# A fused top-k attention and PReLU MLP kernel on one core: one Exp for two duos, score copies two slots ahead, the factor 1 - alpha moved to the Relu, and a new order of the drain

## The chip, the cores and the metric

The kernel runs on one core of one Trainium2 chip. The metric is the device time of one execution in microseconds (us); three runs of the kernel before gave 814.25, 814.66 and 815.23 us, median 814.66. The profile shows one further execution, which took 814.44 us. Engines are named as in the profile: PE (matrix multiply; PEld its weight loads), DVE (vector), ACT (scalar), POOL (GpSimd) and SP (which issues most DMAs; SPq is its queue).

## The reference

Eight batches of eight heads, 576 tokens, head size 64. Each score row keeps its 32 largest entries, the result goes through a two-layer MLP with a PReLU whose slope alpha differs by feature.

```python
def _attn_ref(q, k, v):                       # q, k, v: (8, 8, 576, 64) float32
    scores = scale * np.matmul(q, k.transpose(0, 1, 3, 2))
    kth = np.partition(scores, -top_k, axis=-1)[..., -top_k:-top_k + 1]   # top_k = 32
    scores = np.where(scores >= kth, scores, -1000000000.0)
    attn = np.exp(scores - np.max(scores, axis=-1, keepdims=True))
    attn = attn / (np.sum(attn, axis=-1, keepdims=True) + 1e-09)
    return np.matmul(attn, v).astype(np.float32)

def _moe_ref(x, w_in, w_out, alpha):          # x: (4608, 512), w_in: (512, 2048), w_out: (2048, 512)
    h = x @ w_in
    g = np.maximum(h, 0.0) + alpha * np.minimum(h, 0.0)
    return (g @ w_out).astype(np.float32)
```

## The kernel before

**Work and slots.** Two heads form a pair. The score rows are cut into 144 duos (the list `duos`, lines 77 to 91), each of two tiles of 128 rows by 576 scores: mostly one tile of each head of a pair ("n"), and for the last 64 rows of the heads, one tile of two heads each ("m"). The main loop (lines 736 to 792) runs 144 slots, one per duo; slot n issues one stage for each of several duos, so that the stages of a duo lie slots apart. `stage` (lines 360 to 371) holds the lags. A pair of slots here is an even slot and the odd one after it, and belongs to two duos whose thresholds are found together.

**The stages of duo n.** PE multiplies q by k into the PSUM tile `ps_sc` (`st_qk`, one buffer); ACT copies it to SBUF as `s_sb` (`st_exit`). In slot n DVE takes the eight largest of each of six groups of 96 scores per row (the search, 12 MAX8, results `up` and, in the PSUM tile `small`, `lo`). In odd slots `threshold_steps` folds these for both duos (`fold`, `negate`, `least`, `turn`) into a first threshold `p9`. In slot n + 2 ACT makes the signs against it with a count (`st_count`, tile `sg`), POOL multiplies them with the scores (`st_y`, tile `y`), and DVE takes the next eight with a MAX8 over 576 (`row`, which also writes into `p9`). In slot n + 4 `pick_steps` chooses the exact threshold `KT` from the count, ACT computes Exp (`st_exp`, tile `w`) and the signs against `KT` (`st_cut`, tile `f`), POOL multiplies `w` by `f`, and SP issues a DMA that transposes `w` into `wT`. In slot n + 7 (n + 8 early on) PE multiplies `wT` by v into `xo` (`st_av`), and for each two duos DVE divides by the row sums (`norm_a`, `norm_b`, tile `x`), and SP transposes `x` into `xT`.

**The MLP.** `mlp_ready` cuts finished tokens into units. A unit multiplies `xT` by `w_in_b` into `ph` (`h_pe`), `h_relu` takes Relu of it into `gT`, and parts (`o_pe`) multiply `gT` by `w_out_b` into `pz`, together with `xT` by `w_lin_b`. Since PReLU is alpha h + (1 - alpha) Relu(h), `w_lin_b` is w_in alpha w_out, built in slots 16 to 24, and `w_out_b` carries the factor 1 - alpha: `scale_out` (lines 636 to 644) scales each of its 16 blocks on ACT. `o_act` copies `pz` out, `o_sp` stores it. `keep_warm` fills PE with idle products.

**Order.** Each engine runs its instructions in the order in which this loop issues them (class `Ordered`; all records of the trace carry its line 32, so that groups are told by tile). Only DVE's small steps on the tile `small` float between their neighbours. So a wait at the head of an engine's queue holds all that stands behind it. In a slot ACT has: two signs `sg` with their count reads, sometimes a copy of `pz`, the Exp, two signs `f`, the score copy, sometimes a copy of transposed q or k (`qkT`). The tiles `sg` and `f` share three buffers, `s_sb` has six, `w` four, `wT` three.

**The drain.** After slot 143 the stages that are left are written out by hand (lines 830 to 906), and a loop (907 to 922) empties the MLP, with Relus taken by DVE and ACT in turn. A last check (`check_low`) sets a flag; if it is set, a general path (not run here) repeats the work.

Of the kernel before, what the change touches and what calls it, by code (L numbers as in the profile page):

```python
# [8 lines left out]
FP32 = mybir.dt.float32  # L9
# [8 lines left out]
NG = 6  # L18

# [40 lines left out]
def fast_path(tc, q, k, v, moe_w_in, moe_w_out, moe_alpha, out, flag):  # L60
# [16 lines left out]
    duos = []  # L77
# [15 lines left out]
    with ExitStack() as ctx:  # L93
# [5 lines left out]
        s_p = pool("s", 6)  # L99
# [47 lines left out]
        def sm(ins, reads, writes):  # L147
# [8 lines left out]
            DVE.small.add(ins.ins.name)  # L156
            recent.append((ins.ins, reads, writes))
            del recent[:-60]
# [10 lines left out]
        ws = [const.tile([128, 2, 640], BF16, name=f"w_{i}") for i in range(4)]  # L169
# [3 lines left out]
        alpha1m = const.tile([128, NFT], FP32, name="alpha1m")  # L173
        w_lin_b = [const.tile([128, DMODEL], BF16, name=f"w_lin_b{i}") for i in range(4)]
# [6 lines left out]
        for t in ws:  # L181
            POOL.memset(t[:, :, S:640], 0.0)
# [134 lines left out]
        def dve_slot(n, f_late):  # L317

            norm = norm_of(n)
            rows = duos_at("count", n)  # L320
# [15 lines left out]
            turn = None  # L336
            if n % 2:
                fold, negate, least, turn = threshold_steps(n // 2)
                fold()
                if n < ND - 1:  # L340
                    h_relu()
                negate()
            else:
                h_relu()
            for d in rows:
                row(d, 0)
            if turn:
                least()
                turn()
            if norm:  # L350
                norm_a(norm)
            for d in rows:
                row(d, 1)
            if norm:
                norm_b(norm)
            if f_late:
                h_pe()
                h_relu()
# [6 lines left out]
        for d in range(ND):  # L365
            for kind, lag in (("count", 2), ("cut", 4), ("exp", 4), ("av", 8 if d < 13 else 7)):
                stage.setdefault((kind, d + lag), []).append(d)
        for m in range(ND // 2):
            stage["pick", 2 * m + 4] = [m]
        for d in range(1, ND, 2):  # L370
            stage["norm", d + (8 if d < 13 else 7)] = d

        def st_count(n, rows=(0, 1)):
            s, p9 = T["s", n], T["p9", n // 2]
            if rows[0] == 0:
                T["sg", n] = two.tile([128, 2, S], BF16, name="sg", tag="sg", bufs=3)
                if n % 2 == 0:
                    T["cs", n // 2] = three.tile([128, 4], FP32, name="cs", tag="cs")
            sg, cs = T["sg", n], T["cs", n // 2]
            for i in rows:  # L380
                r = 2 * (n % 2) + i
                ACT.activation(sg[:, i, :], s[:, i, :], AF.Sign, bias=p9[:, r, 0:1], scale=-1.0,
                               accum_out=cs[:, r:r + 1])

        def st_y(n):
            y = two.tile([128, 2, S], FP32, name="y", tag="y")
            sg = T.pop(("sg", n))
            for i in range(2):
                POOL.tensor_tensor(y[:, i, :], T["s", n][:, i, :], sg[:, i, :], ALU.mult)
            T["y", n] = y  # L390
# [4 lines left out]
        def st_cut(n):  # L395
            w, s = ws[n % 4][:, :, 0:S], T.pop(("s", n))
            f = two.tile([128, 2, S], mybir.dt.uint8, name="f", tag="sg", bufs=3)
            for i in range(2):
                ACT.activation(f[:, i, :], s[:, i, :], AF.Sign, bias=KT[:, 2 * n + i:2 * n + i + 1])
# [163 lines left out]
        def h_relu(eng=None):  # L563
            if act:
                ch, f0, e_n, ph = act.pop(0)
                if eng is ACT:
                    ACT.activation(ch["g"][:, f0:f0 + e_n, :], ph, AF.Relu)
                else:
                    DVE.tensor_scalar(ch["g"][:, f0:f0 + e_n, :], ph, 0.0, None, ALU.max)
# [66 lines left out]
        def scale_out(f):  # L636
            if f % 8 == 0:
                hold["wl", f // 8] = gp.tile([128, 8, 512], BF16, name="w_la", tag="gT")
            src = hold["st", f // 4][:, f % 4, :]
            ACT.activation(w_out_b[f // 4][:, f % 4, :], src, AF.Copy, scale=alpha1m[:, f:f + 1])  # L640

            sm(DVE.tensor_tensor(hold["wl", f // 8][:, f % 8, :], src,
                                 alpha_ps[:, f:f + 1].to_broadcast([128, 512]), ALU.mult),
               [(304 + f, 305 + f)], [])
# [91 lines left out]
        for n in range(ND):  # L736
            now[0] = n
            run(n, "kd")
            o_sp()

            if n > 4 and not h_pe():
                keep_warm()
            wide_copy = n % 2 and (n, "prep") in todo
            if n > 3:
                run(n, "prep", 1)
            if n and on(n + 1):
                st_qk(n + 1)
            if n < 4:
                run(n, "prep", 2)
            if 0 < n < 5:  # L750
                keep_warm()
            for m in duos_at("av", n):
                st_av(m)
            late = len(hq) > (9 if n < 118 else 4 if n < 132 else 3) and n % 2 == 0 and not (on(n + 1) and duos[n + 1][0] == "m")

            for m in duos_at("count", n):
                st_count(m)
                st_y(m)
            if ready() > 4 or not wide_copy:
                o_act()  # L760
            for m in duos_at("exp", n):
                st_exp(m)
            if not norm_of(n):
                run(n, "ld")
            run(n, "lin_out")
            did = o_pe()
            run(n, "w")

            dve_slot(n, late)
            for m in duos_at("cut", n):  # L770
                st_cut(m)
            if n and on(n + 1):
                st_exit(n + 1)
            run(n, "cast")
            if (n, "lin") in todo:
                run(n, "lin")
            elif not ready() > (2 if n < 128 else 1) or on(n + 2) and duos[n + 2][0] == "m" or not o_pe():
                if n and not did:
                    keep_warm()
            while pend:  # L780
                short = len(pend[0][0].shape) == 3
                wide = pend[0][0].shape[1] == 512
                on_dve = n > 3 and (short and n > 16 or wide and (n < 17 or n % 2 == 0))
                prep_evac(DVE.tensor_copy if on_dve else ACT.copy)
            if n == 1:
                sm(DVE.tensor_copy(alpha_ps, aps), [], [(304, 320)])
                ACT.activation(alpha1m, aps, AF.Copy, scale=-1.0, bias=1.0)
            run(n, "scale")
            if norm_of(n):
                st_xT(norm_of(n) - 1)  # L790
                st_xT(norm_of(n))
                run(n, "ld")
# [42 lines left out]
        o_sp()  # L835
        st_av(D - 6)
        h_pe(2)
        h_relu(ACT)
        h_pe(2)
        h_relu(ACT)  # L840
        o_act()
        o_sp()
        st_count(D - 1)
        st_y(D - 1)
        picked(D // 2 - 1)
        normed(D - 6)
        h_relu()
        st_count(D)
        st_y(D)
        st_exp(D - 3)  # L850
        st_cut(D - 3)
        st_exp(D - 2)
        row(D - 1, 0)
        now[0] += 1
        o_pe()
        st_av(D - 5)
        o_pe()
        h_pe(2)
        o_pe()
        row(D - 1, 1)  # L860
        h_relu()
        h_pe(2)
        st_av(D - 4)
        row(D, 0)
        row(D, 1)
        st_cut(D - 2)
        picked(D // 2)
        normed(D - 4)
        st_exp(D - 1)
        h_relu(ACT)  # L870
        o_act()
        o_sp()
        h_pe(2)
        o_pe()
        st_exp(D)
        h_relu(ACT)
        st_mask(D - 1)
        st_mask(D)
        st_wT(D - 2)
        o_pe()  # L880
        o_pe()
        o_act()
        o_sp()
        for _ in range(2):
            h_pe(2)
            h_relu(ACT)
        ps = turn_w(D)
        st_av(D - 3)
        turned(D, ps)
        h_pe(2)  # L890
        h_relu(ACT)
        st_av(D - 1)
        st_av(D)
        norm_a(D)
        norm_b(D)
        h_pe(2)
        h_relu(ACT)
        st_av(D - 2)
        normed(D - 2)
        st_xT(D)  # L900
        now[0] += 2
        o_pe()
        o_pe()
        o_pe()
        o_act()
        o_sp()
        turn = 0
        while hq or act or soon or oq or stores:
# [4 lines left out]
            h_relu((DVE, ACT)[turn % 2])  # L913
            turn += 1
            if turn == 1:
                check_low()
            o_act()
            o_sp()
            if not hq and not act:
                o_pe()  # L920
                o_act()
# [282 lines left out]
```

## Time and profile before

| view | value |
|---|---|
| median of three runs | 814.66 us |
| the profiled execution | 814.44 us |
| its span in the trace | 812.4 us |
| busy share of the span | PE 90%, DVE 93%, ACT 94%, POOL 88% |
| clock granted to PE | 0.994 |

The span is from the first to the last instruction; 2.0 us of the execution lie outside it. A busy time counts each instant once, however many records overlap. Groups of instructions are given with count, busy time and mean duration, and with the idle time of the engine ahead of them and what ended it. Two ACT instructions that follow each other without a wait overlap in their records, so the time that one costs is the distance to the start of the next, about 0.1 us less than its record. In the trace slot 2 begins at 17.7 us, slot 18 at 105.9 and slot 142 at 761.7 (first `sg` of the slot).

### The profile page before, as it was taken

The numbers are of one execution on the slowest core, as the hardware profiler recorded it, in microseconds if no ns is written. First come the engines' busy times: TensorE is split into PE (matmuls) and PEld (weight loads), VectorE is DVE, ScalarE is ACT, GpSimd is POOL, SyncE is SP. The second block draws the span as 40 slices with busy tenths as digits, with TensorE's granted clock in tenths as the row PEclk, the third lists the DMA queues.
The fourth block names the chain that finished last, engine by engine and source line by source line (L and its number), as shares of the span: only waits on it lengthen the run. The fifth ranks groups of instructions, "written<-read, shape, count | busy, mean of one in ns | idle before, by whom it ended". The sixth has DMA issues, their size and how long they took to land.

```text
span 812.4 us, 17847 instructions
## 1 busy us (share of the span) xinstructions
PE 734.3 (90%) x5375; PEld 421.4 (52%) x5448; DVE 755.8 (93%) x3470; ACT 767.0 (94%) x1265; POOL 713.6 (88%) x565
## 2 busy tenths in 40 slices
PE   8888899989989998889989989898989999999886
PEld 5333455545545555555545555454545555556563
DVE  4999999999999999999999999999999999999961
ACT  5999999999999999999999999999999999999971
POOL 2898899999999999989999999999999988998860
PEclk9999999999999999999999999999999999999999
DMA  7799976665565575655576555665566565544361
GB/s 153 196 176 173 178 145 133 115 118 116 124 121 122 113 124 120 127 122 105 127 140 117 129 110 124 108 123 117 119 136 116 116 134 100 99 99 89 82 114 37
DMA packets 342327, 99.90 MB, mean 123 GB/s; under 512 B 336128, under 2 KB 336400, under 8 KB 342224
## 3 DMA queue, kind: packets, MB, share of 16 engines
q1 hardware_dynamic: 338928, 91.18, 58.0%
q0 software_dynamic: 1952, 7.09, 3.7%
q8 instruction: 45, 0.74, 0.4%
q10 hardware_dynamic: 1344, 0.43, 0.2%
q14 instruction: 58, 0.48, 0.2%
HBM read 36.71 MB, written 9.44 MB: 57 GB/s over the span
## 4 chain that ended last, share of the span: by engine, by line
DVE 33%; PE 22%; ACT 18%; POOL 12%; issue 10%; SPq 2%; DMA 2%; ACTq 0%; POOLq 0%; DVEq 0%
DVE small L32 11%; PE ps_sc L32 7%; DVE p L32 7%; POOL y L32 7%; DVE up L32 6%; PE pz L32 5%; ACT f L32 5%; ACT sg L32 4%; ACT s_sb L32 4%; POOL w L32 4%; PE ph L32 4%; DVE gT L32 4%; PE xo L32 3%; ACT w L32 3%; SPq L32 2%
## 5 line engine op out<-in xcount | busy, mean ns | idle before, releaser
L32 POOL TENSOR_TENSOR y<-s_sb,sg 128x576 f32<-128x576 f32 x288 | 362.2, 1279 | 25.2 <-ACT sg L32 24.5
L32 POOL TENSOR_TENSOR w<-w,f 128x1152 bf16<-128x1152 bf16 x142 | 317.8, 2238 | 45.8 <-ACT f L32 44.1
L32 ACT ACTIVATE sg<-s_sb,p 128x576 bf16<-128x576 f32 x288 | 221.6, 774 | 10.6 <-DVE p L32 8.3
L32 DVE MAX8 up<-s_sb 128x8 f32<-128x96 f32 x864 | 212.1, 245 | 11.0 <-ACT s_sb L32 10.9
L32 DVE MAX8 p<-y 128x8 f32<-128x576 f32 x288 | 215.0, 748 | 7.3 <-POOL y L32 6.4
L32 DVE MAX8 small<-s_sb 128x8 f32<-128x96 f32 x864 | 216.2, 250 | 0.0
L32 ACT ACTIVATE f<-s_sb,KZ 128x576 uint8<-128x576 f32 x284 | 203.8, 769 | 0.0
L32 PE MATMUL ps_sc<-qkT 64*128 64x512 f32 (+2 forms) x768 | 183.0, 566 | 22.9 <-ACT s_sb L32 22.5
L32 ACT ACTIVATE w<-s_sb 128x1152 bf16<-128x1152 f32 x144 | 166.9, 1159 | 0.0
L32 ACT COPY s_sb<-ps_sc 128x1152 f32<-128x1152 f32 x144 | 159.2, 1106 | 5.8 <-PE ps_sc L32 5.6
L32 PE MATMUL ph<-xT,w_in_b 128*128 128x256 bf16 (+1 forms) x1472 | 149.6, 249 | 7.0 <-DMA xT<-x 3.1
L32 PE MATMUL pz<-w_out_b,gT 128*128 128x512 bf16 x545 | 142.1, 379 | 9.4 <-issue 6.0
L32 PEld LDWEIGHTS <-w_in_b 128*128 128x128 bf16 x1472 | 119.6, 98 | 50.2 <-issue 10.0
L32 PE MATMUL xo<-v,wT 128*128 128x65 bf16 (+3 forms) x1600 | 126.1, 198 | 0.6 <-DVE x L32 0.6
L32 PEld LDWEIGHTS <-wT 128*128 128x128 bf16 (+3 forms) x1600 | 97.3, 99 | 28.9 <-issue 0.8
L32 DVE TENSOR_SCALAR gT<-ph 128x512 bf16<-128x512 f32 x134 | 90.4, 674 | 8.6 <-PE ph L32 8.6
L32 PEld LDWEIGHTS ps_sc<-qkT 64*128 64x128 f32 (+1 forms) x768 | 55.5, 169 | 66.8 <-ACT s_sb L32 35.0
L32 PEld LDWEIGHTS ps_sc<-kd,qkT 128*128 128x128 f32 x256 | 38.1, 188 | 97.1 <-issue 93.3
L32 PEld LDWEIGHTS <-gT 128*128 128x128 bf16 x576 | 54.6, 98 | 59.1 <-DVE gT L32 4.7
L32 PE MATMUL ps_sc<-kd,qkT 128*128 128x128 f32 x256 | 62.5, 326 | 0.0
L32 PE MATMUL rest<-idle 128*128 128x512 bf16 x200 | 52.5, 389 | 6.6 <-DVE gT L32 4.4
L32 ACT ACTIVATION_READ_ACCUMULATOR sg<-s_sb,p 128x1 f32 x288 | 56.2, 195 | 0.0
(67 smaller groups left out, 569.5 us busy)
## 6 DMA issues: line engine op xcount, KB each, us to landing
k_st<-in_k_dram SPq DMA_DIRECT2D x64, 128.0 KB, 2.8
v_st<-in_v_dram SPq DMA_DIRECT2D x64, 128.0 KB, 2.9
q_st<-in_q_dram SPq DMA_DIRECT2D x62, 128.0 KB, 2.7
out_dram<-o_sb SPq DMA_DIRECT2D x29, 256.0 KB, 2.5
w_st<-in_moe_w_out_dram POOLq DMA_DIRECT2D x4, 1024.0 KB, 7.3
wT<-w SPq DMA_TRANSPOSE x143, 3.5
w_in_b<-in_moe_w_in_dram POOLq DMA_DIRECT2D x4, 512.0 KB, 6.6
k_st<-in_k_dram SPq DMA_DIRECT2D x32, 32.0 KB, 2.6
```

Of the source, the lines that this page charges most:

```text
L32: ins = self.tc.keep_in_program_order(f(*a, **kw))
```

## The change

1. **Exp.** `st_exp` of single duos stays for slots 0 to 17 and for the last two duos. From slot 17 on, each odd slot n has one Exp over duos n - 3 and n - 2 (`exp_two`, 128 x 2304), issued behind the two signs `f`. To make that possible the six buffers of `s_sb` become one tile `s_all`, and the four of `w` two tiles `wp` of two duos each.
2. **Copies.** From slot 8 on (`LEAD`) slot n issues the score products and the copy of duo n + 2 rather than n + 1 (`ahead`); slot 8 issues both.
3. **1 - alpha.** `h_relu` becomes one DVE instruction with two inputs, max(ph, 0) times `alpha1m` (an SBUF column repeated along the tokens); `w_out_b` becomes a plain cast of w_out, 11 blocks on ACT and 5 on POOL (`CS`). ACT's Relus of the drain (10) go to DVE.
4. **Loads.** q is loaded at s0 - 4 rather than s0 - 2 (from batch 2 on), v mostly one slot sooner. The lag of 8 for `st_av` ends at duo 10 rather than 12. The pair before the last is prepared one slot sooner; two wide copies of `qkT` go from ACT to DVE.
5. **Order.** A slot is written as a list of names (`HEAD_E`, `HEAD_O` up to slot 17, then `EVEN`, `ODD`), the drain as `DRAIN`. From slot 18 on `st_av` stands ahead of `st_qk` on PE, the copies of `qkT` stand ahead of the Relu on DVE, and `turn` comes behind both `row` steps. `PM` has no "P", `ROWS` is 999 and `SC` has only "D", so these branches are not taken.

```diff
+LEAD = 8
+CS = "AAPAAPAAPAAPAAPA"
+MODE = 18
+PAIRS = 18
+HEAD_E = "kd osp h prep qk av c0 c1 oact exp ld ope S R r0 na r1 nb late k0 k1 exit cast ope2 evac xt"
+HEAD_O = "kd osp h prep qk av c0 c1 oact exp ld ope S F R N r0 L T na r1 nb late E k0 k1 exit cast ope2 evac xt"
+EVEN = "kd osp h prep av c0 c1 oact ld qk ope S evac R r0 na r1 nb late k0 k1 exit cast ope2 xt"
+DRAIN = "a6 osp h RD h RD oact osp c1 p1 n6 RD op c0 k3 r10 h now op a5 r11 RD h a4 r00 r01 op k2 p0 e1 RD oact n4 osp h op e0 m1 RD m0 w2 op op oact osp h RD h RD tw a3 td h RD a1 a0 na nb RD a2 h n2 now now x0 op op oact osp op now h h RD low op oact osp now h h op RD oact osp now h h op RD osp op op oact oact osp"
+ODD = "kd osp h prep av qk ope c0 c1 oact ld S R F r0 N r1 L T late k0 k1 E evac exit cast ope2 xt"
...
-        ws = [const.tile([128, 2, 640], BF16, name=f"w_{i}") for i in range(4)]
+        wp = [const.tile([128, 4, 640], BF16, name=f"w_{i}") for i in range(2)]
+        ws = [wp[i // 2][:, 2 * (i % 2):2 * (i % 2) + 2, :] for i in range(4)]
+        s_all = const.tile([128, 12, S], FP32, name="s_sb")
...
         def st_exit(n):
-            s = s_p.tile([128, 2, S], FP32, name="s_sb", tag="s")
+            s = s_all[:, 2 * (n % 6):2 * (n % 6) + 2, :]
             ACT.copy(s, two_of(T.pop(("ps", n)), 960, S))
...
-            for kind, lag in (("count", 2), ("cut", 4), ("exp", 4), ("av", 8 if d < 13 else 7)):
+            for kind, lag in (("count", 2), ("cut", 4), ("exp", 4), ("av", 8 if d < MODE - 7 else 7)):
...
+        def exp_two(n):
+            c = 2 * (n % 6)
+            ACT.activation(wp[n // 2 % 2][:, :, 0:S], s_all[:, c:c + 4, :], AF.Exp, scale=att_scale)
...
-                if eng is ACT:
-                    ACT.activation(ch["g"][:, f0:f0 + e_n, :], ph, AF.Relu)
-                else:
-                    DVE.tensor_scalar(ch["g"][:, f0:f0 + e_n, :], ph, 0.0, None, ALU.max)
+                DVE.scalar_tensor_tensor(out=ch["g"][:, f0:f0 + e_n, :], in0=ph, scalar=0.0,
+                                         in1=alpha1m[:, f0:f0 + e_n].unsqueeze(2).to_broadcast(list(ph.shape)),
+                                         op0=ALU.max, op1=ALU.mult)
...
-                s0 = NB * (b - 1) + 4 + 4 * i + (2 if p == NPAIR - 2 else 0)
+                s0 = NB * (b - 1) + 4 + 4 * i + (1 if p == NPAIR - 2 else 0)
                 at(s0 - 3, "ld", lambda p=p: load_one(p, "k"))
-                at(s0 - 2, "ld", lambda p=p: load_one(p, "q"))
+                at(s0 - (2 if b == 1 else 4), "ld", lambda p=p: load_one(p, "q"))
                 early = 2 if b == B - 1 else 0
-                at(s0 + 6 - early, "ld", lambda p=p: load_one(p, "v"))
+                at(s0 + (6 if b == 1 and i < 2 else 5) - early, "ld", lambda p=p: load_one(p, "v"))
...
-            ACT.activation(w_out_b[f // 4][:, f % 4, :], src, AF.Copy, scale=alpha1m[:, f:f + 1])
+            plain = w_out_b[f // 4][:, f % 4, :]
+            if CS[f] == "A":
+                ACT.copy(plain, src)
+            else:
+                POOL.tensor_copy(plain, src)
...
+        def ahead(n):
+            return [m for m in ([n + 1] if n < LEAD else [n + 1, n + 2] if n == LEAD else [n + 2]) if n and on(m)]
...
+            def t_E():
+                if n % 2 and n >= PAIRS - 1 and on(n - 3):
+                    exp_two(n - 3)
...
+            for t in ((HEAD_O if n % 2 else HEAD_E) if n < MODE else ODD if n % 2 else EVEN).split():
+                tok[t]()
...
-        o_sp()
-        st_av(D - 6)
-        h_pe(2)
-        h_relu(ACT)
...
+        for t in DRAIN.split():
+            end[t]()
         while hq or act or soon or oq or stores:
             now[0] += 1
             while h_pe(2):
                 pass
             o_pe()
-            h_relu((DVE, ACT)[turn % 2])
+            h_relu()
```

The names stand for: c0, c1 the count and `y` of one row tile each; k0, k1 the signs `f` and, behind k1, POOL's product and the transpose; exp, E the single and the double Exp; exit the score copy; S the search; F, N, L, T `fold`, `negate`, `least`, `turn`; R and RD the Relu; r0, r1 `row`; na, nb the division; evac the copies of `qkT`; oact, osp copy and store of the output; ope, op a part, h a unit of the MLP; ld, xt the loads and the transposes of `x`. In the drain a number is the duo counted back from the last one (a6 is `st_av` of the last but six, r10 its first row tile of the last but one).

More of the change, by code (lines that the diff above doesn't have):

```diff
@@ L392, in st_exp, with st_cut @@
         def st_exp(n):
             ACT.activation(ws[n % 4][:, :, 0:S], T["s", n], AF.Exp, scale=att_scale)
[L395 to L399, printed above, removed]
+        def st_cut(n, rows=(0, 1)):
+            w, s = ws[n % 4][:, :, 0:S], T["s", n]
+            if rows[0] == 0:
+                T["f", n] = two.tile([128, 2, S], mybir.dt.uint8, name="f", tag="sg", bufs=3)
+            f = T["f", n]
+            for i in rows:
+                kt = KT[:, 2 * n + i:2 * n + i + 1]
+                if i and MODE < now[0] < ND - 4 and PM[now[0] % 18] == "P":
+                    POOL.tensor_scalar(f[:, i, :], s[:, i, :], kt, 0.0, ALU.add, ALU.is_gt)
+                else:
+                    ACT.activation(f[:, i, :], s[:, i, :], AF.Sign, bias=kt)
+            if rows[-1] == 0:
+                return
@@ L734, in fast_path, with evac @@
         PE.transpose(aps, a16, ident_f[0:NFT, 0:NFT])
-        for n in range(ND):
-            now[0] = n
-            run(n, "kd")
-            o_sp()
[L741 to L779, printed above, removed]
+        def ahead(n):
+            return [m for m in ([n + 1] if n < LEAD else [n + 1, n + 2] if n == LEAD else [n + 2]) if n and on(m)]
+        def evac(n):
             while pend:
@@ L782, in fast_path @@
                 wide = pend[0][0].shape[1] == 512
-                on_dve = n > 3 and (short and n > 16 or wide and (n < 17 or n % 2 == 0))
+                on_dve = n > 3 and (short and n > 16 or wide and (EV[n] == "D" if n < 18 else n % 2 == 0))
                 prep_evac(DVE.tensor_copy if on_dve else ACT.copy)
[L785 to L788, printed above, removed]
@@ L794, in picked, with is_late @@
+        def is_late(n):
+            return len(hq) > (9 if n < 118 else 4 if n < 132 else 3) and n % 2 == 0 and not (on(n + 1) and duos[n + 1][0] == "m")
+        for n in range(ND):
+            slot(n)
         def picked(m):
@@ L858, in fast_path @@
[L858 to L907, printed above, removed]
+        turn = []
+        def end_now():
+            now[0] += 1
@@ L912, in fast_path @@
             o_pe()
[L913 to L916 removed]
+            h_relu()
             o_act()
             o_sp()
[L919 to L921 removed]
         o_sp()
```

238 lines of the change are left out of this document (168 added, 70 removed).

## The prediction

> **What bounds the kernel now.** I read the busy shares first, then the stages, then what each engine waits for, then one slot of ACT in order of time.
>
> ```profile
> span 812.4 us, 17847 instructions
> core 0: us, PE busy (x) PEld busy (x) DVE busy (x) ACT busy (x) POOL busy (x), PEclk, DMA share, GB/s
> 20.00:104.00 84.00, 70.67 (x396) 32.74 (x395) 79.99 (x354) 82.43 (x141) 77.08 (x68) 0.96 0.94 179
> 104.00:762.00 658.00, 606.46 (x4486) 351.10 (x4551) 641.04 (x2976) 645.72 (x1056) 610.22 (x454) 1.00 0.60 118
> 762.00:812.40 50.40, 39.33 (x411) 26.15 (x415) 25.79 (x82) 27.13 (x47) 21.67 (x18) 0.97 0.40 76
> ```
>
> The three stretches are the head (slots up to 17), the steady part and the drain. In the steady part ACT is busy 645.7 of 658 us, DVE 641.0, POOL 610.2: ACT idles 12.3 us, DVE 17.0. Two engines are full, and each waits a little for the other:
>
> ```profile
> ACT sg L32 <- DVE p L32: 8.3, 21, 1.7
> DVE up L32 <- ACT s_sb L32: 6.2, 20, 0.7
> DVE gT L32 <- PE ph L32: 2.8, 5, 1.0
> POOL w L32 <- ACT f L32: 40.0, 65, 1.1
> L32 ACT COPY s_sb<-ps_sc 128x1152 f32<-128x1152 f32 x125 | 138.0, 1104 | 1.7 <-PE ps_sc L32 1.5
> L32 ACT COPY o_sb<-pz 128x512 f32<-128x512 f32 x31 | 17.5, 566 | 0.0
> ```
>
> (Wait rows: us in total, times, longest.) ACT's sign waits for `turn`, DVE's search for the score copy. POOL's waits cost nothing by themselves. The 125 score copies give 125 slots, 5.26 us each, 10.53 us for an even and an odd slot, and 62 such pairs of slots.
>
> ```profile
> 310.09 1.10 ACT L32 COPY s_sb<-ps_sc 128x1152 f32<-128x1152 f32 x1
> 311.09 0.78 ACT L32 ACTIVATE sg<-s_sb,p 128x576 bf16<-128x576 f32 x1
> ...
> 312.62 1.15 ACT L32 ACTIVATE w<-s_sb 128x1152 bf16<-128x1152 f32 x1
> 313.67 1.43 ACT L32 ACTIVATE f<-s_sb,KZ 128x576 uint8<-128x576 f32 x2
> 315.00 1.10 ACT L32 COPY s_sb<-ps_sc 128x1152 f32<-128x1152 f32 x1
> ```
>
> From start to start: copy 1.00, two signs `sg` 1.53, Exp 1.05, two signs `f` 1.33 us.
>
> **One Exp for two.** The two copies above have slopes (1104 - 566) / 640 = 0.84 ns per column. An Exp of 2304 columns then takes 1.15 + 1152 x 0.84 ns = 2.12 us of record and some 2.02 to its successor, against 2 x 1.05: 0.08 us saved for a pair of slots, 5 us over 62. The other bound: `f` (1.43 us for two, 0.76 one) and Exp (1.15) give 0.68 ns per column, hence 0.27 us saved, 17 us. I take the copies, which differ only in length, while `f` reads `KZ` besides.
>
> The Trainium skill ("ScalarE: Activation LUTs", What ACT_TABLE_LOAD costs) puts an activation without a pointer operand at 186 ns + 0.833 ns per column, one with a pointer about 93 ns higher, and lets neighbours overlap by some 93 ns. It speaks against the change: only the 93 ns that do not overlap would be saved, 6 us in all, and `f`'s higher record would be its pointer.
>
> **What the copies cost ACT.** In the built program the copy of duo n + 2 waits for the second `f` of duo n - 4, whose buffer it takes. In even slots that `f` is the instruction right in front of it; in odd slots the Exp lies between. Such a wait on a neighbour shows here:
>
> ```profile
> 13.12 0.27 ACT L32 COPY qkT<-tps 128x128 f32<-128x128 f32 x1
> 13.47 0.50 ACT L32 COPY kd<-qkT 64x64 f32<-64x64 f32 x2
> ...
> 312.83 0.24 DVE L32 MAX8 up<-s_sb 128x8 f32<-128x96 f32 x1
> 312.99 0.25 DVE L32 MAX8 small<-s_sb 128x8 f32<-128x96 f32 x1
> 313.28 0.25 DVE L32 TENSOR_TENSOR bot<-up,small 128x96 f32<-128x96 f32 x1
> ```
>
> The second copy starts 0.08 us after the first ends; without the wait it would start 0.1 us before that end. So 0.18 us in each even slot, 11 us over 62, unless the write of `f` is known sooner (0). On DVE the same form costs 0.29 - 0.16 = 0.13 us, and there it goes away: the Relu now stands between the last MAX8 and `bot`, 8 us less on DVE.
>
> **What the copies gain.** The search no longer waits for a copy of the slot before (6.2 us), so `turn` comes early enough for the next sign (8.3 us). I check that it does, counting from an even slot's first sign: `y` of that slot is ready at 0.77 + 1.28 = 2.1 us, and DVE wants it after its search (2.2) and the Relu (0.6); the odd slot's second `y` is ready at about 8.5, behind two `y` (2.5), `w` (2.2), a cast (0.4) and two more `y` on POOL; its `row` and `least` (0.67 + 0.6) end at 9.8, before ACT is through at about 10.4. So ACT sets the pace, and the sum is ACT's: 645.7 - 5 + 11 = 651.7 of 658 without any idle time. Each wait that goes also restores an overlap of 0.1 us (23 waits, 2 us). **Steady part: -7 us** (0 if waits stay, -17 at most if the new wait on `f` costs nothing).
>
> **The Relu.** DVE's new form has not run here. Its neighbours:
>
> ```profile
> L32 DVE TENSOR_SCALAR gT<-ph 128x512 bf16<-128x512 f32 x134 | 90.4, 674 | 8.6 <-PE ph L32 8.6
> L32 DVE TENSOR_TENSOR w_la<-w_st,small 128x512 bf16<-128x512 f32 x16 | 10.5, 675 | 0.0
> L32 DVE TENSOR_TENSOR small<-small,cs 128x36 f32<-128x36 f32 x72 | 13.3, 184 | 0.0
> L32 DVE SCALAR_TENSOR_TENSOR pk<-small,p 128x36 f32<-128x36 f32 x72 | 12.9, 179 | 0.1
> L32 DVE SCALAR_TENSOR_TENSOR w<-s_sb,KZ,w 128x576 bf16<-128x576 f32 x4 | 4.8, 1262 | 0.0
> ```
>
> `pk` has the new form's make, one input from PSUM (`small`) and one from SBUF, and costs no more than the plain product beside it (179 against 184 ns); the product over 512 with one PSUM input takes 675 ns, as the Relu does. So 0, with the masks' 1262 ns for two SBUF inputs as the other bound (a rival below).
>
> **Head.** 16 scaled blocks leave ACT; 11 casts come in, 5 go to POOL.
>
> ```profile
> L32 ACT ACTIVATE w_out_b<-w_st,alpha1m 128x512 bf16<-128x512 f32 x16 | 11.4, 742 | 0.0
> L32 POOL CAST v<-v_st 128x256 bf16<-128x256 f32 x64 | 25.3, 399 | 0.0
> ```
>
> A cast from SBUF is the Exp less 640 columns, 1.15 - 0.54 = 0.61 us of record. ACT: 16 x 0.64 - 11 x 0.51 = 4.6 us less; the new wait on `f` in the ten slots from 8 to 17 gives 1.8 back. POOL pays 5 x about 0.6 = 3 us and had 6.9 idle of 84; DVE had 4.0 idle, which limits what a lighter ACT brings. **Head: -2 us** (+1 to -3). q and v loaded sooner, fewer `keep_warm`: 0, since no engine's large wait is on a load.
>
> **Drain.**
>
> ```profile
> 766.30 2.24 POOL L32 TENSOR_TENSOR w<-w,f 128x1152 bf16<-128x1152 bf16 x1 [1.10 <-ACT f L32]
> 771.21 2.24 POOL L32 TENSOR_TENSOR w<-w,f 128x1152 bf16<-128x1152 bf16 x1 [0.20 <-ACT f L32]
> 778.59 4.44 POOL L32 TENSOR_TENSOR w<-w,f 128x1152 bf16<-128x1152 bf16 x2
> ...
> 772.64 1.07 PE L32 MATMUL ph<-xT,w_in_b 128*128 128x128 bf16 x16 [1.98 <-DMA xT<-x]
> 785.79 1.96 PE L32 MATMUL ph<-xT,w_in_b 128*128 128x128 bf16 x32 [1.14 <-DMA xT<-x]
> 805.13 0.81 PE L32 MATMUL pz<-w_out_b,gT 128*128 128x512 bf16 x3
> ```
>
> ACT has no copy in the last two slots, two Exp fewer ahead of the last signs, and no Relu, so POOL's waits of 1.10 and 0.20 us go, and all behind them comes 1.3 us sooner. PE runs nearly without gaps from 785.79 to its end; its gaps of 1.98 and 1.14 are what a better order could fill. Relus (0.6 us net on DVE) queue behind the four masks (4.8 us). **Drain: -3 us** (+2 to -4).
>
> Sum: 814.4 - 7 - 2 - 3 = **802.4 us**. The profiled execution lies 0.2 us below the median of the runs.
>
> **Rivals.**
>
> *The pair's Exp waits for transposes (slower).* `w` now holds two pairs, so the Exp of an odd slot waits until the transposes of the pair before the last have landed.
>
> ```profile
> 304.55 2.24 POOL L32 TENSOR_TENSOR w<-w,f 128x1152 bf16<-128x1152 bf16 x1
> 309.76 1.38 SPq L32 DMA_TRANSPOSE wT<-w  x1
> DMA to landing us min/median/max: 3.3/3.5/9.8
> ```
>
> The product here ends at 306.79 in an odd slot's turn; the new Exp of the next odd slot would start at 311.09 + 1.53 + 1.33 = 313.95, 7.2 us later. SP issued the transpose 3.0 us late, behind loads, and 3.5 us pass to landing: 6.5. For: 0.7 us to spare, landings up to 9.8, and v, k and q loads now lie in a row on SP between transposes. Against: where SP is free it is 3.6. Every 0.1 us of mean wait costs 6 us; from 0.2 us a pair on the change is a loss. At 0.3 us: 802 + 19 = 821.
>
> *The Relu runs at the masks' rate (slower).* 2.03 ns per column rather than 1.15 net: 1.1 us against 0.59, 0.5 us x 144. DVE's 641 us of the steady part grow by 129 x 0.5 to 705, less 8: 697, 39 above 658; with the head and the drain about 855. Against it stands `pk`.
>
> By the Trainium skill ("Vector Engine (DVE) Microarchitecture Reference", Points that are easy to get wrong) this form halves its throughput with two SBUF sources that are not bf16; the masks go at half rate with one source bf16. With `ph` in PSUM the rule leaves the Relu at full rate.
>
> *The steady part stays (no gain there).* `turn`, now behind both rows, still comes late, and ACT goes on waiting 8 us; with 11 more for the copies nothing is left: 814.4 - 5 = 809.
>
> *No price for the wait on `f`* (the larger gain): 802 - 9 = 793.
>
> **How the numbers follow.** Forecast 0.56, steady part stays 0.21, no price 0.10, transposes 0.10, slow Relu 0.03. The likeliest one's own range is 797 to 808. For 8 in 10 I take 793 to 814, which cuts the slow cases and the tail of the fast one. No change is within 0.2%, 813.0 to 816.3. Faster: 0.56 + 0.10 + 0.19 of the 0.21 = 0.85, less 0.02 for the forecast's tail: 0.83. Slower: 0.13. Same: 0.04.
>
> **What would show it.** In the changed kernel's steady part: some 10.4 us between first signs of even slots; ACT busy over 98.5%; `up` no longer waiting for `s_sb`, signs seldom for `p`; the copy in even slots starting about 0.08 us after `f` ends, in odd slots 0.1 before the Exp ends; the Exp of 2304 columns near 2.1 us; the Relu near 675 ns. Wrong would be: the Exp idle behind a DMA, Relus over 1 us, DVE waiting for `y` in most slots, or POOL busy over 97% in the head.

## The result, and the profile after

The changed kernel takes 810.88 us, the median of 5 runs (809.68 to 811.20), beside 814.74 us for the kernel before in 5 runs (814.25 to 816.76): a ratio of 0.9944, 95% interval 0.9928 to 0.9959 (taken over all runs; the two medians alone give 0.9953). That is 3.9 us less, where the forecast had 12.3. The direction was right and the time lies in the range, but the likeliest case's own range (797 to 808) does not hold it. The profiled execution took 809.68 us, with a span of 807.9 us beside 812.4. One run among those told of below, 3689.79 us of the version "one ahead, single Exp", was in a slow state and has no part in its median and ratio.

I cut the span at the first sign `sg` of slot 18 and of slot 142. The first fence is the kernel before, the second the changed one; the columns are the stretch, its length, and the busy time of each engine.

```profile
core 0: us, PE busy (x) PEld busy (x) DVE busy (x) ACT busy (x) POOL busy (x), PEclk, DMA share, GB/s
17.71:105.88 88.17, 74.84 (x419) 35.15 (x420) 83.20 (x371) 86.53 (x147) 80.30 (x70) 0.96 0.92 177
105.88:761.72 655.84, 604.30 (x4469) 349.94 (x4534) 638.92 (x2968) 643.57 (x1053) 608.06 (x453) 1.00 0.60 119
761.72:812.40 50.68, 39.61 (x416) 26.33 (x418) 26.07 (x82) 27.40 (x47) 21.95 (x18) 0.97 0.40 75
```

```profile
core 0: us, PE busy (x) PEld busy (x) DVE busy (x) ACT busy (x) POOL busy (x), PEclk, DMA share, GB/s
17.50:110.87 93.37, 79.41 (x443) 37.31 (x444) 85.84 (x387) 87.08 (x145) 83.19 (x75) 0.95 0.85 172
110.87:759.27 648.40, 593.48 (x4457) 349.97 (x4523) 632.46 (x2955) 640.12 (x989) 608.18 (x453) 1.00 0.60 119
759.27:807.90 48.63, 38.40 (x394) 26.26 (x398) 31.44 (x91) 18.93 (x33) 21.23 (x17) 0.95 0.40 79
```

The head is 5.2 us longer (93.37 against 88.17; forecast 2 shorter), the steady part 7.4 shorter (forecast 7), the drain 2.0 shorter (forecast 3). So the question is the head. There ACT has about as much to do as before (87.08 against 86.53 us) but is idle for 6.3 us rather than 1.6. Its two large gaps up to slot 18 that the kernel before does not have, and one in slot 21, are these rows of ACT in order of time (start, duration, instruction, and in brackets the idle time before it and what ended it):

```profile
50.79 1.42 ACT L45 ACTIVATE f<-s_sb,KZ 128x576 uint8<-128x576 f32 x2
52.12 1.09 ACT L45 COPY s_sb<-ps_sc 128x1152 f32<-128x1152 f32 x1
56.16 1.12 ACT L45 COPY s_sb<-ps_sc 128x1152 f32<-128x1152 f32 x1 [2.95 <-PE ps_sc L45]
...
103.78 1.15 ACT L45 ACTIVATE w<-s_sb 128x1152 bf16<-128x1152 f32 x1
105.89 2.12 ACT L45 ACTIVATE w<-s_sb 128x2304 bf16<-128x2304 f32 x1 [0.96 <-DMA wT<-w]
...
130.44 2.12 ACT L45 ACTIVATE w<-s_sb 128x2304 bf16<-128x2304 f32 x1 [1.76 <-DMA wT<-w]
```

At 52.12 is slot 8, where the copies take their lead: one slot makes two score products and two copies. There is one PSUM buffer `ps_sc`, so the second product waits for the first copy and the second copy for the second product. At 105.89 is slot 17, where the pair's Exp begins, one slot after single Exps: this slot has both, and the large one stands ahead of the signs `f`. At 130.44 is slot 21; its Exp waits for a transpose that stood on SP behind loads. PE in slot 8:

```profile
53.27 2.08 PE L45 MATMUL ps_sc<-qkT 64*128 64x512 f32 x4 [2.76 <-ACT s_sb L45]
55.27 0.80 PE L45 MATMUL ps_sc<-kd,qkT 128*128 128x128 f32 x2
```

The steady part, one odd and one even slot of ACT:

```profile
309.06 1.10 ACT L45 COPY s_sb<-ps_sc 128x1152 f32<-128x1152 f32 x1
310.14 0.77 ACT L45 ACTIVATE sg<-s_sb,p 128x576 bf16<-128x576 f32 x1
...
312.14 1.44 ACT L45 ACTIVATE f<-s_sb,KZ 128x576 uint8<-128x576 f32 x2
313.61 1.12 ACT L45 COPY s_sb<-ps_sc 128x1152 f32<-128x1152 f32 x1
314.62 0.78 ACT L45 ACTIVATE sg<-s_sb,p 128x576 bf16<-128x576 f32 x1
...
316.15 1.43 ACT L45 ACTIVATE f<-s_sb,KZ 128x576 uint8<-128x576 f32 x2
317.49 2.11 ACT L45 ACTIVATE w<-s_sb 128x2304 bf16<-128x2304 f32 x1
```

The even slot's copy (313.61) starts 0.03 us after the `f` ahead of it ends (312.14 + 1.44); the `f` at 316.15 is followed 0.09 us before its end. The groups that answer the forecast's prices, and the waits between 110 and 760 us:

```profile
L45 ACT ACTIVATE w<-s_sb 128x2304 bf16<-128x2304 f32 x64 | 135.1, 2112 | 2.9 <-DMA wT<-w 2.9
L45 DVE SCALAR_TENSOR_TENSOR gT<-ph,alpha1m 128x512 bf16<-128x512 f32 x144 | 97.5, 678 | 6.7 <-PE ph L45 6.7
L45 ACT CAST w_out_b<-w_st 128x512 bf16<-128x512 f32 x11 | 6.6, 621 | 0.0
L45 POOL CAST w_out_b<-w_st 128x512 bf16<-128x512 f32 x5 | 3.0, 608 | 0.0
```

```profile
DVE p L45 <- POOL y L45: 11.7, 30, 2.6
...
ACT sg L45 <- DVE p L45: 2.2, 4, 0.7
ACT s_sb L45 <- PE ps_sc L45: 2.1, 3, 0.8
ACT w L45 <- DMA wT<-w: 1.9, 2, 1.8
```

`up` has left the list, and the signs wait 2.2 us for `p` where they waited 8.3.

### The profile page after: what moved, and what is told of

Its sections match the earlier page's. It is cut to its first block, busy times and chain, and to the rows that moved or that the text cites. A ratio compares the mean times of both kernels' runs of the same rounds, so it can differ in the third digit from the quotient of the medians.

```text
span 807.9 us, 17825 instructions
## 1 busy us (share of the span) xinstructions
PE 725.9 (90%) x5368; PEld 422.8 (52%) x5440; DVE 757.5 (94%) x3482; ACT 755.7 (94%) x1185; POOL 715.8 (89%) x568
## 4 chain that ended last, share of the span: by engine, by line
DVE 48%; ACT 15%; PE 14%; POOL 12%; issue 9%; DMA 1%; SPq 0%; ACTq 0%; DVEq 0%; POOLq 0%
DVE small L45 14%; DVE p L45 14%; POOL y L45 10%; DVE up L45 8%; ACT sg L45 7%; DVE gT L45 5%; PE ps_sc L45 4%; PE pz L45 4%; ACT f L45 4%; PE ph L45 3%; ACT s_sb L45 3%; POOL w L45 2%; PE xo L45 2%; DVE x L45 2%; DVE qkT L45 2%
## 5 line engine op out<-in xcount | busy, mean ns | idle before, releaser
L45 PE MATMUL ps_sc<-qkT 64*128 64x512 f32 (+2 forms) x768 | 180.6, 565 | 21.4 <-ACT s_sb L45 21.2
L45 ACT ACTIVATE w<-s_sb 128x2304 bf16<-128x2304 f32 (+1 forms) x80 | 153.6, 1920 | 2.9 <-DMA wT<-w 2.9
L45 PEld LDWEIGHTS <-wT 128*128 128x128 bf16 (+3 forms) x1600 | 94.4, 99 | 57.1 <-issue 23.5
L45 DVE SCALAR_TENSOR_TENSOR gT<-ph,alpha1m 128x512 bf16<-128x512 f32 x144 | 97.5, 678 | 6.7 <-PE ph L45 6.7
L45 PEld LDWEIGHTS ps_sc<-qkT 64*128 64x128 f32 (+1 forms) x768 | 53.2, 169 | 49.0 <-ACT s_sb L45 26.1
```

The costliest lines, as they stand in the source:

```text
L45: ins = self.tc.keep_in_program_order(f(*a, **kw))
```

## The experiments

Where a stage is disputed I read the slots from the trace of each run. The table gives the median of the runs, the ratio to the kernel before with its 95% interval, and three stretches between first signs `sg`: slots 2 to 28 (the head and what follows from it), 28 to 118 (45 pairs of slots), and 142 to the end of the span. Where two kernels do the same work, pairs of slots from 28 on mostly agree within 0.01 us between traces, so that the stretch 28 to 118 resolves more than the medians do. Slots 2 to 28 hold two things that differ between executions of the same instructions. One is the wait for a transpose ahead of the Exp of slot 17. In the four traces that have the same instructions up to that Exp (the changed kernel, one q load later, all q loads later, copy behind the sign) it is 1.0, 2.4, 2.1 and 2.6 us. So the changed kernel's trace has this wait at its least. The other is the wait of ACT's second copy in slot 8: 2.95 us in these four traces, but 1.92 where only the Exp of slot 17 was moved, since the product ahead of it ran there at the full clock (see the last section). In this column differences below 2 us decide nothing by themselves.

| kernel | median us | ratio to before | slots 2 to 28 | 28 to 118 | 142 to end |
|---|---|---|---|---|---|
| before | 814.74 | 1 | 141.02 | 473.16 | 50.6 |
| changed | 810.88 | 0.9944 (0.9928 to 0.9959) | 147.53 | 466.17 | 48.6 |
| first copy of slot 8 early | 808.90 | 0.9918 (0.9906 to 0.9931) | 146.06 | 466.77 | 48.4 |
| Exp of slot 17 behind `f` | 808.94 | 0.9924 (0.9909 to 0.9939) | 146.18 | 466.19 | 48.7 |
| one q load later | 809.38 | 0.9930 (0.9918 to 0.9942) | 147.08 | 466.12 | 49.5 |
| these three | 806.32 | 0.9893 (0.9878 to 0.9907) | 143.92 | 466.67 | 48.7 |
| two single Exp | 812.67 | 0.9965 (0.9949 to 0.9980) | 145.42 | 471.06 | 49.6 |
| copy behind the sign | 804.43 | 0.9860 (0.9845 to 0.9874) | 148.61 | 460.87 | 48.6 |
| 1 - alpha on w_out | 813.19 | 0.9966 (0.9953 to 0.9979) | 151.99 | 466.16 | 49.6 |
| copies one ahead | 814.57 | 1.0004 (0.9983 to 1.0025) | 146.16 | 471.64 | 48.7 |
| one ahead, single Exp | 815.60 | 1.0006 (0.9985 to 1.0028) | 144.05 | 473.73 | 49.6 |
| all casts on ACT | 811.62 | 0.9953 (0.9938 to 0.9969) | 150.23 | 465.78 | 49.1 |
| all q loads later | 816.60 | 1.0020 (1.0007 to 1.0033) | 146.83 | 471.54 | 49.5 |
| three edits and copy behind the sign | 800.52 | 0.9824 (0.9811 to 0.9837) | 142.33 | 461.51 | 48.6 |

My theory after reading the result: the steady part is as forecast, and the head loses what it costs to take the two leads, which the forecast had not priced. The rival: the head is full of work on DVE and POOL, and ACT's idle time there would come back in any case.

**First copy of slot 8 early.**

```diff
 t_qk:    -  for m in ahead(n): st_qk(m)
          +  for m in ahead(n)[:1]: st_qk(m)
 t_oact:  +  if n == LEAD: st_exit(n + 1); st_qk(n + 2)
 t_exit:  -  for m in ahead(n): st_exit(m)
          +  for m in ahead(n)[-1:]: st_exit(m)
```

> In slot 8, where the copies gain their lead, the first score copy comes in the middle of the slot (behind the output copy's place) and the second score product behind it, so that the two copies at the end need not wait for each other. Theory H (the head's loss lies in idle time at the places where the lead is taken): ACT's wait of 2.95 us at 56.16 goes, slots 8 to 10 take about 12.7 us instead of 15.07, and 2.4 us go from the whole, 808.5 us beside 810.9 for the changed kernel. Rival W (the head is full of work on DVE and POOL, so that idle time on ACT comes back as another wait before slot 18): slot 18 still starts at 110.9, total 810.5 to 811.3. Rival S (only the work moved forward counts, a copy of 1.0 us): slots 8 to 10 get shorter by less than 1 us, total about 810.

The whole falls by 2.0 us, near the 2.4 of theory H, and slots 8 to 10 take 13.45 us rather than 15.08: the wait of 2.95 us is 1.17 ahead of the first copy. Part of such a difference can be the execution's, but the ranges lie apart: in the three traces with this edit ACT's wait in slot 8 is 0.8 to 1.2 us, in those that take the lead without it 1.7 to 2.95. But in this trace slot 18 starts at 110.81, as the rival had it. ACT of this run:

```profile
51.41 1.12 ACT L45 COPY s_sb<-ps_sc 128x1152 f32<-128x1152 f32 x1 [1.17 <-PE ps_sc L45]
...
105.83 2.12 ACT L45 ACTIVATE w<-s_sb 128x2304 bf16<-128x2304 f32 x1 [2.54 <-DMA wT<-w]
```

The Exp of slot 17 waits 2.54 us here. That is within what it waits with nothing changed ahead of it (1.0 to 2.6), so the trace alone does not tell whether the stall of slot 8 went there; what holds the head at that place is a DMA, not DVE or POOL. The medians decide for H: all runs of this version (807.53 to 809.16 us) lie below all of the changed kernel.

**Exp of slot 17 behind `f`.**

```diff
-HEAD_O = "... late E k0 k1 exit ..."
+HEAD_O = "... late k0 k1 E exit ..."
```

> In the odd slots before 18 the place of the pair's Exp is behind the signs f instead of ahead of them; only slot 17 has one. Theory H: the wait of 0.96 us for the transpose ahead of this Exp goes and POOL's product no longer waits 3.09 us for f; ACT keeps the 2.0 us of work moved forward; slots 16 to 18 take about 12.7 us instead of 13.68, total 809.9. Rival W: nothing that can be seen, 810.5 to 811.3.

Slots 16 to 18 take 13.32 us, less of a gain than expected; the wait for the transpose is still 0.74 us. Of the 1.6 us that this trace gains from slot 2 to 18, 1.0 lies in slot 8, where nothing was changed. The median falls by 1.9 us, twice the forecast, which was made from the one trace with a short wait.

**One q load later.**

```diff
-at(s0 - (2 if b == 1 else 4), "ld", ...)
+at(s0 - (2 if p < 9 else 4), "ld", ...)
```

> The q load of the third batch's first pair of heads goes back from four slots ahead to two, out of the row of transposes that the Exp of slot 21 waits for. Theory T (the pair's Exp waits for transposes that stand behind loads on SP): the wait of 1.76 us ahead of the Exp at 130.44 shrinks below 0.5 us, slots 20 to 22 take about 10.8 us instead of 12.23, total 809.5. Rival: the transpose is late because of the w_inT transpose and the kd copies as well, and the wait stays above 1.2 us, total 810.5 to 811.3.

Slots 20 to 22 take 10.36 us rather than 12.23, as expected, with no wait left there. But the q load is not all of the 1.76 us: with the three edits below it stands behind these transposes too, and the Exp of slot 21 waits 1.22 us, while with the first copy early, and q in its old place, it waits 0.37. The median fell by 1.5 us, though the Exp of slot 17 waited 2.4 us in this trace.

**These three together.**

> The three edits together: first copy in the middle of slot 8, pair's Exp behind f in slot 17, q of the third batch's first pair two slots ahead. Theory H with T: 2.4 + 1.0 + 1.4 = 4.8 us, slot 18 at about 107.5 instead of 110.87, slot 28 at about 160.2 instead of 165.03, total about 806. Rival W: slot 28 stays past 163.5, total above 809.5.

806.32 us, as the theory had it: slot 18 starts at 107.80, slot 28 at 161.41. In slot 8 PE is held up for 0.55 us only; its second product, the counterpart of the row at 53.27 above:

```profile
51.77 1.13 PE L45 MATMUL ps_sc<-qkT 64*128 64x512 f32 x4 [0.55 <-ACT s_sb L45]
```

Slots 16 to 18 still take 12.98 us against 10.29 before, with 0.41 us of waiting: what is left is the work moved forward, two single Exp's worth.

**Two single Exp for the pair's.**

```diff
-ACT.activation(wp[n // 2 % 2][:, :, 0:S], s_all[:, c:c + 4, :], AF.Exp, ...)
+for i in (0, 2):
+    ACT.activation(wp[n // 2 % 2][:, i:i + 2, 0:S], s_all[:, c + i:c + i + 2, :], AF.Exp, ...)
```

> The pair's Exp of 2304 columns becomes two Exp of 1152 at the same place. The prediction's price, 0.08 us for a pair of slots: slots 28 to 118 take 469.8 us instead of 466.2, the whole +5, about 816. The other bound, 0.27 us: 478.3, the whole +17. Rival (ACT's time is not what sets the pace there): below +1 us in slots 28 to 118.

Slots 28 to 118 take 4.9 us more: 0.11 us for a pair of slots, near the price of 0.08 and far from 0.27. The Trainium skill ("ScalarE: Activation LUTs", What ACT_TABLE_LOAD costs) gives neighbours an overlap of 93 ns out of a fixed 186, which would make it 0.093 us, 4.2 in this stretch; the run agrees within 0.7. In ACT's rows, each counted to the start of the next one or to its own end if that is sooner, the Exp of this stretch take 94.8 us rather than 90.6: 4.2 us, 0.093 for a pair. The rest of the 4.9 lies in waits. The median rose by 1.8 us only, in runs from 810.48 to 816.04; in this trace slots 2 to 28 were 2.1 us shorter.

**Copy behind the sign.** The copy that waits on its neighbour gets one instruction between.

```diff
-EVEN = "... k0 k1 exit cast ..."
-ODD  = "... av qk ope c0 c1 oact ..."
+EVEN = "... k0 k1 cast ..."
+ODD  = "... av c0 X qk ope c1 oact ..."
+def t_X():
+    if n > MODE and on(n + 1): st_exit(n + 1)
```

> From slot 18 on, the copy of an even slot moves behind the first sign sg of the odd slot after it, so that it no longer stands right behind the f whose buffer it takes; the score product behind it on PE moves likewise. Theory (the wait on the neighbour costs ACT 0.13 us for a pair of slots, by the 0.03 us gap and the 0.1 us of lost overlap in the profile): slots 28 to 118 take 460 to 463 us instead of 466.2, the whole -4 to -8, about 803 to 807. Rival N (the wait costs nothing, because the buffer's last read would end then anyway): 466. Rival P (POOL and DVE, at 95% and 98.5%, take up the time at once, or the later product delays the odd slot's copy): 465 to 468.

460.87 us, inside the theory's interval: 5.3 us less, 0.12 for each pair. ACT of this run:

```profile
312.06 1.44 ACT L45 ACTIVATE f<-s_sb,KZ 128x576 uint8<-128x576 f32 x2
313.40 0.76 ACT L45 ACTIVATE sg<-s_sb,p 128x576 bf16<-128x576 f32 x1
314.06 0.19 ACT L45 ACTIVATION_READ_ACCUMULATOR sg<-s_sb,p 128x1 f32 x1
314.16 1.10 ACT L45 COPY s_sb<-ps_sc 128x1152 f32<-128x1152 f32 x1
```

The sign starts 0.10 us before `f` ends, and the copy 0.09 before the accumulator's read ends. The rivals N and P fall: the wait had a price, and POOL and DVE could follow.

**1 - alpha back on w_out.**

```diff
-DVE.scalar_tensor_tensor(out=ch["g"][...], in0=ph, scalar=0.0, in1=alpha1m[...], op0=ALU.max, op1=ALU.mult)
+DVE.tensor_scalar(ch["g"][...], ph, 0.0, None, ALU.max)
-ACT.copy(plain, src)  or  POOL.tensor_copy(plain, src)
+ACT.activation(plain, src, AF.Copy, scale=alpha1m[:, f:f + 1])
```

> 1 - alpha goes back from the Relu to w_out: 16 scaled copies on ACT in the head in place of 11 casts there and 5 on POOL, and a plain Relu on DVE. The prediction's terms: the Relu costs the same in either form, so slots 28 to 118 stay within 1 us of 466.2; in the head ACT has 4.6 us more and POOL 3 us less, slot 28 comes 2 to 4.6 us later (167 to 169.6), the whole +2 to +4.6. Rival (POOL's casts or the Relu with two inputs cost as much as ACT saves): slot 28 within 1 us of 165.0, the whole within 1 us of 810.9.

Slots 28 to 118 take 466.16 against 466.17 us: the two forms of the Relu cost the same. Slots 2 to 28 take 4.5 us more, of which ACT's busy time is 3.6 (142.96 against 139.32 us) and its waits 0.8. Counted to the start of the next one, the 16 scaled copies take 9.9 us here and the 11 casts 5.7 in the changed kernel: 4.2 us, near the forecast's 4.6. The median rose by 2.3 only.

**All casts on ACT.**

```diff
-CS = "AAPAAPAAPAAPAAPA"
+CS = "AAAAAAAAAAAAAAAA"
```

> All 16 casts of w_out on ACT, none on POOL. The prediction's terms: 5 x 0.51 us more on ACT, which sets the head's pace: slot 16 comes about 2 us later than 97.19 and slot 18 than 110.87, the whole +1.5 to +2.6. Rival (POOL is what the head waits for): slot 16 earlier by up to 2 us.

Slot 16 comes only 0.5 us later, but the wait in slot 8 is 1.3 us shorter in this trace (1.69 us), so its place does not tell the price. Slots 2 to 28 take 2.7 us more: 2.2 of work on ACT and 0.5 of waiting, with 3.20 us ahead of the Exp of slot 17. The median rose by 0.7 only. By the medians, then, five casts on POOL gain 0.7 us, not the 2.5 that ACT's count gives; where the rest goes is not shown.

**Copies one ahead to the end.**

```diff
-LEAD = 8
+LEAD = 999
```

> The copies stay one slot ahead to the end (the lead is never taken); all else is as in the changed kernel. Theory (the lead costs 1.0 us of moved work and up to 2.95 us of idle time at slot 8, and gains in every pair of slots by the waits it removes): slots 8 to 10 take about 11.7 us; slots 28 to 118 take 470 us instead of 466.2, since DVE's search waits for the copy and ACT's sign for turn again; the end comes about 2 us later after slot 142, the whole 812 to 814. Rival (the lead is worth nothing, the gain of the steady part is the Exp's alone): slots 28 to 118 within 1 us of 466.2, the whole 806 to 808.

Slots 28 to 118 take 471.64 us, 5.5 more. Between 165 and 631 us these two waits are back, which the changed kernel does not have there:

```profile
DVE up L45 <- ACT s_sb L45: 9.7, 23, 0.8
ACT sg L45 <- DVE p L45: 3.9, 12, 0.4
```

The end comes 48.7 us after slot 142 rather than 48.6: the drain does not gain from the copies' lead, though the theory had 2 us for it. Nor does the head get shorter by what the lead costs there: slots 2 to 28 take 146.16 us, with ACT idle for 9.1 us (8.2 in the changed kernel), 3.17 of it ahead of the Exp of slot 17 and 2.1 behind DVE in slot 10. So the rival of a full head may be right in part: idle time that goes in one place can come back in another.

**Copies one ahead and single Exp.** Both edits together.

> Both undone: copies one slot ahead to the end, and two Exp instead of the pair's. Undone alone, each cost 5 us in slots 28 to 118 (466.2 to 471.1 and to 471.6). Theory (they lie one behind the other on ACT, and add): 476.5 us in slots 28 to 118, which means that the rest of the new order costs 3 us there beside the kernel before (473.15). Rival (without the lead ACT has idle time, and the Exp's saving falls into it): 472 to 474 us, as the kernel before.

473.73 us: the rival is right. Undone one at a time, each costs about 5 us, undone together 7.6. Without the lead ACT has idle time, and the Exp's saving falls into it: beside the run before, the single Exp add 4.3 us of work to ACT in slots 28 to 118 and take 2.2 us off its idle time there (8.4 to 6.1).

**All q loads later.**

```diff
-at(s0 - (2 if b == 1 else 4), "ld", ...)
+at(s0 - 2, "ld", ...)
```

> All q loads back at two slots ahead. The prediction put the move of the q loads at 0. Theory: slots 28 to 118 within 1 us of 466.2, with the one wait at slot 21 shorter as before, the whole 809 to 811. Rival (q loaded late holds up the transposes on PE, and the score copies behind them): slots 28 to 118 above 467.5.

This edit alone brings the time back above that of before, 816.60 us, with 5.4 us in slots 28 to 118, and neither as the theory nor by the way that the rival named. The first fence is ACT of this run, the second SP's queue ahead of it, the third SP of the changed kernel at the same place:

```profile
632.41 2.12 ACT L45 ACTIVATE w<-s_sb 128x2304 bf16<-128x2304 f32 x1 [2.39 <-DMA wT<-w]
```

```profile
622.41 1.80 SPq L45 DMA_DIRECT2D q_st<-in_q_dram  x3
624.26 1.24 SPq L45 DMA_DIRECT2D kd<-qkT  x2
625.54 1.83 SPq L45 DMA_DIRECT2D v_st<-in_v_dram  x3
627.49 7.00 SPq L45 DMA_TRANSPOSE wT<-w  x3
```

```profile
620.22 1.22 SPq L45 DMA_DIRECT2D kd<-qkT  x2
621.48 1.86 SPq L45 DMA_DIRECT2D v_st<-in_v_dram  x3
623.45 4.41 SPq L45 DMA_TRANSPOSE wT<-w  x2
```

With q in the row, the transposes stand behind 5.0 us of other issues (622.41 to 627.37) rather than 3.1, and the pair's Exp waits 2.39 us. It does so in few pairs: of the 45, those at slots 70, 106 and 116 lose 1.6, 1.0 and 2.5 us and two more 0.3 each, where nearly all others are equal.

**The three edits of the head and the copy behind the sign.**

> The three edits of the head and the copy behind the sign together. If the gains add (4.6 us beside the changed kernel for the head's three, 5.3 us in slots 28 to 118 for the copy): slot 28 at about 161.5, slots 28 to 118 in 461 us, the whole 798 to 801. Rival (the copy moved behind the sign in slot 18 on lets the Exp of slots 17 and 21 wait longer, as the early copy in slot 8 did by itself): slot 28 past 164, the whole above 802.5.

800.52 us, 0.9824 of the kernel before (0.9811 to 0.9837) and 10.4 us below the changed kernel: the gains add. Slot 28 starts at 159.87, and in this trace the Exp of slot 17 does not wait at all. This version beats both kernels.

## Why the prediction was right, and where it was not

**The step that failed is the head** ("Head: -2 us (+1 to -3)"; measured +5.2 to slot 18, +6.5 from slot 2 to 28). The terms it had were near: ACT's 4.6 us less were 4.2, and the waits on `f` cost ACT 1.5 where 1.8 stood (the signs `f` take 33.5 us of its time from slot 2 to 28, 32.0 before). It had no term for taking the leads. Two of those were to be had from the diff and the rows of before:

- Work moved forward. The copies lead by one slot more (1.0 us) and the Exp by two duos (2 x 1.05 us), so ACT does 3.1 us more ahead of slot 18 and as much less in the drain. The forecast counted the gain, in the drain ("ACT has no copy in the last two slots, two Exp fewer"), but not the price.
- Idle time at the switch: 2.95 us in slot 8 through the single `ps_sc` buffer, of which 1.0 is the halved clock. The waits for transposes, 0.96 in slot 17 and 1.76 in slot 21, come from SP's queue. From slot 2 to 28 ACT was idle for 8.2 us, 2.1 before.

Together: -4.2 + 3.1 + 6.1 + 1.5 = 6.5, the whole. That most of the idle time was to be had back is shown: the three edits took 4.6 us off the median. How much of it belongs to which place is not shown, since without the copies' lead the head keeps its idle time elsewhere. The moved work was priced from ACT's rows only; slots 16 to 18 with the three edits (12.98 us, 0.41 of it waiting, 10.29 before) fit it. "DVE had 4.0 idle, which limits what a lighter ACT brings" was the wrong limit: DVE was idle for more after the change (93.37 - 85.84 = 7.5 us). Why the transpose of slot 17 lands up to 1.6 us later in one execution than in another is open.

**The steady part** was right in sum (-7; 7.4 from slot 18 to 142) and in its pace: 466.17 / 45 = 10.36 us for a pair, ACT busy 98.7%. Its parts were not. The sum had 6 us more work on ACT and its 12.3 us of idle time gone; measured were 3.4 less work and 4.0 less idle (12.3 to 8.3). In ACT's rows from slot 18 to 142, each counted to the start of the next one or to its own end, the Exp take 6.0 us less (131.0 to 125.0; forecast 5) and the signs `f` 6.5 more (165.6 to 172.1), which nearly cancel. The whole wait on `f` costs 0.12 us for a pair of slots rather than 0.18, of which the gap is 0.03 and not 0.08: the short copies of `kd` that served as the row overstate it. The rest of the 3.4 lies mostly in the wide copies of `qkT`, 13.8 us before and 10.7 after. Two of 25 went to DVE; 16 of the 25 stood before right ahead of a sign that had to wait, and lost their overlap, which none does now. That is about what the forecast had for waits that go (2 us): with copies one ahead, where signs and search wait again, the score copies and the accumulator's reads take 2.1 us more in slots 28 to 118. That the gains hang together, the forecast had only as a rival ("the steady part stays").

**The q loads** stood at 0, "since no engine's large wait is on a load". The waits would have been on transposes behind the loads. Loading q sooner is worth 5.4 us of the steady part, and is why *the pair's Exp waits for transposes* did not come true there; at the start, in slots 17 and 21, it did, for 2.7 us in the profiled execution. The rival was the right mechanism, with its cure in the diff.

**The Relu** cost nothing, as forecast: 678 ns and equal stretches. Its rival falls.

**The drain** gave 2.0 of 3 us. From the first sign of slot 142 to the end of POOL's last product the row of before gives 778.59 + 4.44 - 761.73 = 21.30 us, and the changed kernel, on POOL,

```profile
767.46 2.24 POOL L45 TENSOR_TENSOR w<-w,f 128x1152 bf16<-128x1152 bf16 x1
...
774.86 4.44 POOL L45 TENSOR_TENSOR w<-w,f 128x1152 bf16<-128x1152 bf16 x2
```

774.86 + 4.44 - 759.27 = 20.03: 1.3 us, the forecast's figure, though not through the copy, since the kernel with copies one ahead reaches the same. PE's order behind it gave 0.7 rather than 1.7. Which of the steps of the drain did it was not tried by itself.

**No price for the wait on `f`** falls with the copy behind the sign, and points the way: the price was avoidable by one instruction between.

## What to carry to other kernels

When a pipeline is made one stage deeper, price its start: the work pulled ahead of the bottleneck's first full slot, and the buffer that must serve twice in the slot of the switch; the drain pays it back only as far as the same engine sets the drain. Two savings on one engine can hang together, so undo each alone and both together before adding them. Where an instruction waits for the one right ahead of it on its engine and loses the overlap (here 0.12 us each time on ACT), move another one in between.

## What the runs showed of the hardware

In slot 8 of the changed kernel PE waits 2.76 us, and the granted clock is halved before the wait ends (from 52.5 us on). The stretch 53 to 57 us of the changed kernel:

```profile
53.00:57.00 4.00, 3.73 (x17) 1.85 (x18) 3.54 (x11) 1.05 (x2) 3.89 (x5) 0.50 0.60 91
```

The clock is 0.50 there, and the four products of `ps_sc` took 2.08 us; with a wait of 0.55 us, in the run with the three edits, 1.13. So the gap cost a second time, 0.95 us in these products; the two at 55.27 took 0.80 rather than 0.49. The half clock does not come at the same place in every execution. With only the Exp of slot 17 moved, PE waits 2.76 us in slot 8 as well, but the clock is 1.00 up to 54.80 us and 0.50 from there to 58.22, so that these four products still run at the full rate:

```profile
53.63 1.13 PE L45 MATMUL ps_sc<-qkT 64*128 64x512 f32 x4 [2.76 <-ACT s_sb L45]
```

An earlier wait of PE, 2.14 us long, is followed by a clock of 0.50 in the run with the first copy early (from 43.52 us) and by none in the run with the three edits. The Trainium skill ("TensorE: Matmul & The Clock Gate", Part 1: The HAM clock gate) puts the step down to half rate behind an idle window of about 3.4 us; here a shorter gap was enough.
